# Attention and two expert layers on one core: the fourth pair's last chunks two a turn, and eight early conversion calls

## The chip, the cores and the metric

The kernel runs on one core of a Trainium2 chip. The metric is device time in microseconds (us), the median of several runs. Five engines work side by side: TensorE (PE, whose weight loads are shown as PEld), VectorE (DVE), ScalarE (ACT), GpSimd (POOL) and SyncE (SP). Each takes its own instructions strictly in the order in which they stand in its queue and waits where an input is not ready. DMA transfers are issued from the queues of SP and of ACT (shown as SPq and ACTq).

## What is computed

Attention over 4 batches of 8 heads (576 tokens, head size 64), with a threshold on the scores, then two feed-forward layers over 2304 tokens (width 512, hidden width 2048):

```python
scores = scale * np.matmul(q, k.transpose(0, 1, 3, 2))
thresh = np.max(scores, axis=-1, keepdims=True) - tau
scores = np.where(scores >= thresh, scores, -1000000000.0)
attn = np.exp(scores - np.max(scores, axis=-1, keepdims=True))
attn = attn / (np.sum(attn, axis=-1, keepdims=True) + 1e-09)
x = np.matmul(attn, v)                      # heads side by side: 2304 x 512
h = x @ w_in;  r = np.maximum(h, 0.0)
x = (s * (r * r) + b) @ w_out               # first experts
h = x @ w_in2; g = h * np.tanh(softplus(h))
out = g @ w_out2                            # second experts
```

The weights arrive as 64-bit floats. Each is turned into a high and a low 32-bit part, and a matrix product is made of three products (high by high, high by low, low by high).

## The kernel before

The heads are taken in 16 pairs; four pairs make one batch. A pair has 9 tiles of scores (tile 4 holds rows of both heads), and the generator `attention` runs in turns k, one tile of scores in each: pair k // 9, tile k % 9. Counted from 0, the fourth pair is pair 3. For each tile PE makes the scores S (`scores`, line 346), DVE takes the row maximum while copying them to ns (L350), ACT the exponential (L358), DVE applies the threshold and sums (`finish`, L364), and POOL normalises (L374). Seven turns (LAG) after its scores, chunk c of the pair is transposed on PE into the only buffer T (`weights_t`, L387 and L392) and copied to te by ACT (L398). One T is free again only when its copy has been made. The products with v stand in two runs for each pair (`products_v`, L414 and L417): chunks 1, 4, 0 one turn after the transpose of chunk 6, and chunks 3, 2 one turn after that of chunk 8. Then `split_x` writes the pair's output x as a high part xh (ACT, L425) and a low part xl (DVE, L426). While the scores of pair 4 and 5 are worked on, the transposes of pair 3 are made.

The first experts take a batch once its four pairs have their x: `moe1(0)` needs xh and xl of pairs 0 to 3. Its accumulators h (L516) take nine products from pairs 0 to 2, and the last three from pair 3.

The weights of the first experts are converted in the same time by `split_all`, a chain of `split_w` pieces. A piece loads wraw (L62 on SP while the start-up pool `s2p` is open, L64 on ACT after it was closed), scales it on ACT (L71), puts the bits together on DVE into wa (L73 to L75), casts the high part wp on ACT (L78) and subtracts for the low part (L79, on POOL while `s2p` is open, else on DVE). The result is also stored to memory (L200 on SP). The order of SP is kept behind the pair's moves: L62 is issued after the last move of K or Q made by then (L307). One step of this chain is made at each call `next(w1)`: ahead of the experts at the turns listed in AHEAD (15, 20, 24, 29, 33, 38, 42), and inside `moe1(0)` at every fourth of its yields, the first one among them.

`run` takes attention alone until x of pair 3 exists (in turn 43), then closes `s2p` and interleaves attention and experts by the costs that the generators yield. The order of each engine is not that of the code: a scheduler picks from what is ready, by the position in the code (attention with a priority of 200 positions) and its own estimates of time.

Of the kernel before, what the change touches and what calls it, by code (L numbers as in the profile page):

```python
# [19 lines left out]
class Fused:  # L20
# [409 lines left out]
    def attention(self):  # L430

        nc = self.nc
        self.turn = 0
        N = 9 * self.B * self.NP
        LAG = 7
        for n in "kq":
            self.load_raw(0, n)
        nc.sync.dma_start(self.tau_c, self.tau.partition_broadcast(P))  # L440
        nc.sync.dma_start(self.s_c, self.s.partition_broadcast(P))
        nc.sync.dma_start(self.b_c, self.b.partition_broadcast(P))
        for pr in range(2):
            self.load_raw(pr, "v")
        warm = self.pvp.tile([P, 1024], F32, tag="pv", name="warm")[:, :512]
        self.busy(warm[:, :256], 20)
        self.prep_first(lambda n: self.busy(warm[:, :256], 2 * n))
        fin = todo = None
        tes = {}
        for k in range(N + LAG + 2):  # L450
            pr, ti = divmod(k, 9)
            self.turn = k
            if k < N:
                nxt = self.scores(pr, ti)
                if k < 12:
                    self.busy(warm[:, :256], 3)
                if fin:
                    fin()
                fin = nxt
                yield 550  # L460
                if pr + 1 == self.B * self.NP and ti == 2:
                    self.load_raw(pr, "v")
                if pr + 1 < self.B * self.NP and ti in (1, 4):
                    self.prep_qk(pr + 1, "kq"[ti // 4])
                    if ti == 4 and pr >= 2:
                        with self.tc.issue_after(self.moved):
                            self.load_raw(pr, "v")
                    yield 500
            elif fin:
                fin()  # L470
                fin = None
            j = k - LAG
            run = None
            if todo:
                tp, tc, te = todo
                tes[tc] = te
                if tc == 6:
                    run = self.products_v(tp, (1, 4, 0), tes, True, False)
                    yield 1460
                elif tc == 8:  # L480
                    run = self.products_v(tp, (3, 2), tes, False, True)
                    yield 970
                    self.split_x(tp)
            todo = None
            if 0 <= j < N:
                prj, ci = divmod(j, 9)
                todo = prj, ci, self.weights_t(prj, ci, run)
                yield 550

    def acc(self, name):  # L490
# [297 lines left out]
    def run(self, ctx):  # L788
        tc = self.tc
# [27 lines left out]
        while 3 not in self.x:  # L817
            next(att)
            if self.turn > done and self.turn in AHEAD:
                next(w1)  # L820
# [6 lines left out]
        def first():  # L827

            for i, c in enumerate(self.moe1(0)):
                if i % 4 == 0:  # L830
                    next(w1, None)
                yield c

# [46 lines left out]
        for i, c in enumerate(self.moe1(3)):  # L880
            if 16 <= i < 64 and i % 2:
                next(comb, None)
            elif i >= 64 and i % 4 == 0:
                next(first, None)
# [11 lines left out]


EARLY = 14
AHEAD = [15] + [9 * pr + ti for pr in (2, 3, 4) for ti in (2, 6)]
HALVES = [slice(0, 64), slice(64, 128)]  # L900

N2 = 384
# [48 lines left out]
```

## Time and profile before

| | |
|---|---|
| median of 3 runs | 1115.9 us (1115.75 to 1117.29) |
| the profiled execution | 1117.13 us, of which 1114.9 us are the span from first to last instruction |
| PE busy | 1073.3 us, 96% of the span |
| DVE, ACT, POOL busy | 792.9, 624.9, 285.1 us |
| mean granted TensorE clock | 0.995 |

A busy PE is read with care: the ends of matmuls are modelled, and pipelined matmuls of 288 columns start about every 0.13 us though each is shown with about 0.3 us. What counts is where PE stands idle or has a lower clock. That is for the greater part in the first 130 us, in which attention runs without the experts. From about 132 us on the experts' products fill every hole.

Engines are also slow or fast by their neighbours: the same instruction on DVE or POOL is longer in some places than in others.

### The profile page before, as it was taken

The numbers are of one execution on the slowest core, as the hardware profiler recorded it, in microseconds if no ns is written. First come the engines' busy times: TensorE is split into PE (matmuls) and PEld (weight loads), VectorE is DVE, ScalarE is ACT, GpSimd is POOL, SyncE is SP. The second block draws the span as 40 slices with busy tenths as digits, with TensorE's granted clock in tenths as the row PEclk, the third lists the DMA queues.
The fourth block names the chain that finished last, engine by engine and source line by source line (L and its number), as shares of the span: only waits on it lengthen the run. The fifth ranks groups of instructions, "written<-read, shape, count | busy, mean of one in ns | idle before, by whom it ended". The sixth has DMA issues, their size and how long they took to land.

```text
span 1114.9 us, 21378 instructions
## 1 busy us (share of the span) xinstructions
PE 1073.3 (96%) x7964; PEld 1012.0 (91%) x7964; DVE 792.9 (71%) x1662; ACT 624.9 (56%) x1189; POOL 285.1 (26%) x354
## 2 busy tenths in 40 slices
PE   7987899999999999899999989999999999999998
PEld 6766789999899999879999879999999999999998
DVE  5989699998556777878757656735695468725782
ACT  5777687585486575577746667634453245413451
POOL 4556454355072351344515201100000000000000
PEclk9999999999999999999999999999999999999999
DMA  7577588785666879969855599968998999997783
GB/s 165 132 179 218 149 269 243 237 256 178 196 182 216 259 220 285 306 202 310 305 177 196 184 368 359 357 224 311 349 393 314 364 418 380 342 333 255 261 288 119
DMA packets 141590, 292.69 MB, mean 263 GB/s; under 512 B 52848, under 2 KB 78960, under 8 KB 133168
## 3 DMA queue, kind: packets, MB, share of 16 engines
q1 hardware_dynamic: 127104, 277.93, 74.0%
q10 hardware_dynamic: 14384, 13.40, 4.1%
q8 instruction: 63, 1.03, 0.4%
q14 instruction: 39, 0.32, 0.1%
HBM read 201.85 MB, written 66.58 MB: 241 GB/s over the span
## 4 chain that ended last, share of the span: by engine, by line
PE 70%; DVE 5%; DMA 5%; POOL 2%; issue 2%; ACT 1%; SPq 0%; ACTq 0%; DVEq 0%; POOLq 0%
PE o L761 16%; PE y L516 14%; PE h L516 12%; PE qY L627 7%; PE qX L627 5%; PE qV L627 4%; PE S L346 4%; PE pv L417 3%; PE T L387 3%; DMA wsi<-chli 2%; DMA w<-w 2%; POOL e L374 1%; DMA wso<-chlo 1%; PE pv L414 1%; DVE ns L350 1%
## 5 line engine op out<-in xcount | busy, mean ns | idle before, releaser
L761 PE MATMUL o<-wo,hl 128*128 128x256 f32 x1512 | 177.7, 279 | 0.0
L761 PEld LDWEIGHTS o<-wo,hl 128*128 128x128 f32 x1512 | 177.4, 188 | 0.0
L516 PE MATMUL h<-xh,w 128*128 128x288 f32 x768 | 164.6, 299 | 2.2 <-ACT xh L425 0.7
L516 PE MATMUL y<-gh,w 128*128 128x288 f32 x768 | 164.8, 299 | 1.3 <-DVE y L563 0.8
L374 POOL TENSOR_SCALAR e<-e,st 128x576 f32<-128x576 f32 x128 | 140.5, 1109 | 34.0 <-DVE st L369 24.7
L350 DVE TENSOR_SCALAR_CACHE_REDUCE ns<-S 128x576 f32<-128x576 f32 x144 | 108.0, 752 | 43.9 <-PE S L346 43.0
L358 ACT ACTIVATE e<-ns,st 128x576 f32<-128x576 f32 x128 | 98.9, 775 | 71.1 <-DVE ns L350 67.8
L364 DVE SCALAR_TENSOR_TENSOR e<-ns,st,e 128x576 f32<-128x576 f32 x128 | 114.1, 895 | 26.4 <-ACT e L358 22.9
L516 PEld LDWEIGHTS h<-xh,w 128*128 128x128 f32 x768 | 126.0, 188 | 3.7 <-ACT xh L425 1.2
L516 PEld LDWEIGHTS y<-gh,w 128*128 128x128 f32 x768 | 126.3, 188 | 2.5 <-DVE y L563 1.4
L398 ACT COPY te<-T 128x576 f32<-128x576 f32 x144 | 91.2, 633 | 50.2 <-PE T L392 45.1
L540 POOL TENSOR_TENSOR gl<-rr,gh 128x288 fp32r<-128x288 f32 x96 | 90.3, 952 | 108.9 <-ACT rr L539 107.8
L516 PE MATMUL h<-xl,w 128*128 128x288 f32 x384 | 113.7, 296 | 0.0
L516 PE MATMUL y<-gl,w 128*128 128x288 f32 x384 | 113.4, 295 | 0.0
L346 PE MATMUL S<-KH,Q 128*128 128x288 f32 x320 | 96.2, 318 | 15.7 <-DVE ns L350 7.3
L387 PE MATMUL T<-ident,e 128*128 128x128 f32 x576 | 90.9, 278 | 7.2 <-ACT te L398 5.0
L387 PEld LDWEIGHTS T<-ident,e 128*128 128x128 f32 x576 | 68.0, 142 | 24.2 <-issue 13.6
L346 PE MATMUL S<-KL,Q 128*128 128x288 f32 x320 | 89.9, 297 | 0.0
L627 PE MATMUL qY<-yc,wi 128*128 128x384 f32 x432 | 86.6, 337 | 1.3 <-DVE g L650 1.3
L417 PE MATMUL pv<-te,rawv 128*64 128x288 f32 x576 | 87.8, 423 | 0.0
L346 PEld LDWEIGHTS S<-KH,Q 128*128 128x128 f32 x320 | 60.6, 190 | 21.7 <-DVE ns L350 10.5
L627 PEld LDWEIGHTS qY<-yc,wi 128*128 128x128 f32 x432 | 75.6, 188 | 1.9 <-DVE g L650 1.9
(151 smaller groups left out, 2204.1 us busy)
## 6 DMA issues: line engine op xcount, KB each, us to landing
w<-w SPq DMA_DIRECT2D x96, 512.0 KB, 5.4
wo<-wso SPq DMA_DIRECT2D x42, 1024.0 KB, 7.1
wi<-wsi SPq DMA_DIRECT2D x23, 1024.0 KB, 8.2
wi<-wsi SPq DMA_DIRECT2D x25, 768.0 KB, 8.0
w<-wp SPq DMA_DIRECT2D x32, 512.0 KB, 4.7
wsi<-chli SPq DMA_DIRECT2D x24, 512.0 KB, 4.8
wso<-chlo SPq DMA_DIRECT2D x24, 512.0 KB, 7.1
ycd<-yp SPq DMA_DIRECT2D x14, 768.0 KB, 7.6
```

What stands on the lines that cost most here:

```text
L346: self.scored = nc.tensor.matmul(so, Q[:, c0:c0 + 128], kt[:, ks], start=(i == 0), stop=(i == len(terms) - 1)).ins
L350: nc.vector.tensor_scalar(ns.rearrange("p (h n) -> p h n", h=2), sv, -0.125, 3.0e38, op0=ALU.mult, op1=ALU.min, accum_out=nm[:, c1])
L358: nc.scalar.activation(e, ns, AF.Exp, bias=nm[:, c1], scale=-1.0)
L364: nc.vector.scalar_tensor_tensor(e, ns, nthr[:, c1], e, op0=ALU.is_le, op1=ALU.mult, accum_out=sm[:, c1])
L374: nc.gpsimd.tensor_scalar(t, t, rinv[:, j:j + 1], u[:, j:j + 1], op0=ALU.mult, op1=ALU.add)
L387: nc.tensor.transpose(T[:, i * 128:i * 128 + 128], self.es[pr, i, "pair"][:, o:o + 128], self.ident)
L398: nc.scalar.copy(te, T[:, :576])
L417: ins = self.nc.tensor.matmul(*args, **kw).ins
L516: nc.tensor.matmul(acc[:, :n], w[:, wl, c], rhs[c][xl][:, ts], start=(i == 0), stop=(i == 11))
L540: (nc.vector if b == 3 else nc.gpsimd).tensor_tensor(gl[:, ts], r2, gh[:, ts].bitcast(F32), op=ALU.subtract)
L627: self.nc.tensor.matmul(acc, a, b, start=(first and i == 0), stop=(i == n - 1), skip_group_check=True)
L761: nc.tensor.matmul(bank[p][t], hl[:, gl, j, ts], w[:, 2 * (q % 2) + j, wl], start=(old is None and q + j + k == 0), stop=(q + j + k == 6), ...
```

## The change

Two things are changed. In turns 39 and 40 two chunks are transposed in each (5 and 6, then 7 and 8 of pair 3: the numbers 32 to 35), and none in turns 41 and 42. The first run of products of pair 3 is thereby written in turn 40 (before: 41), the second one in turn 41 (before: 43), and `run` leaves its start-up loop in turn 42. RUNS holds the same two runs as before for every pair, since SOLO is 0. And the conversion is called at eight turns ahead of the experts (15, 19, 23, 27, 31, 35, 39, 42) in place of seven; the call at the first yield of `moe1(0)` is left out, so that the count inside the experts is the same at each later yield.

```diff
-        fin = todo = None
-        tes = {}
+        fin, todo, tes = None, [], {}
+        soon = {39: (32, 33), 40: (34, 35), 41: (), 42: ()} if TWO else {}
+
+        def due(k):
+            return soon.get(k, (k - LAG,) if 0 <= k - LAG < N else ())
+
...
-            j = k - LAG
             run = None
-            if todo:
-                tp, tc, te = todo
+            for tp, tc, te in todo:
                 tes[tc] = te
-                if tc == 6:
-                    run = self.products_v(tp, (1, 4, 0), tes, True, False)
-                    yield 1460
-                elif tc == 8:
-                    run = self.products_v(tp, (3, 2), tes, False, True)
-                    yield 970
+                for chunks in RUNS[tp < SOLO].get(tc, ()):
+                    run = self.products_v(tp, chunks, tes, chunks == RUNS[tp < SOLO][min(RUNS[tp < SOLO])][0], tc == 8)
+                    yield 486 * len(chunks)
+                if tc == 8:
                     self.split_x(tp)
-            todo = None
-            if 0 <= j < N:
+            todo = []
+            for j in due(k):
                 prj, ci = divmod(j, 9)
-                todo = prj, ci, self.weights_t(prj, ci, run)
+                todo.append((prj, ci, self.weights_t(prj, ci, run)))
+                run = None
                 yield 550
...
-                if i % 4 == 0:
+                if i and i % 4 == 0:
                     next(w1, None)
...
-AHEAD = [15] + [9 * pr + ti for pr in (2, 3, 4) for ti in (2, 6)]
+SOLO = 0
+TWO = True
+RUNS = ({6: [(1, 4, 0)], 8: [(3, 2)]}, {5: [(0, 4)], 6: [(1,)], 7: [(2,)], 8: [(3,)]})
+AHEAD = [15, 19, 23, 27, 31, 35, 39, 42]
```

What the scheduler makes of it is seen in the order of the engines. In these rows the number behind a name's last underline is only a counter of tiles; the digit ahead of it is the tile of scores or the chunk (T_6 and te_6 belong to chunk 6).

**Place 1.** ACT where pair 2 ends and the transposes of pair 3 begin. Before (wraw_1290 is the sixth piece of weights):

```order
L398 COPY te_8_1149<-T_8_1143 128x576
L78 CAST wp_0_3_1013<-wa_1417 128x512
L78 CAST wp_1_0_1135<-wa_1605 128x512
L425 CAST xh_1169<-pv_1104 128x576
L398 COPY te_0_1179<-T_0_1173 128x576
L358 ACTIVATE e_2_1272<-ns_2_1269,st_1199 128x576
L398 COPY te_1_1197<-T_1_1191 128x576
L358 ACTIVATE e_3_1309<-ns_3_1306,st_1199 128x576
L71 ACTIVATE wraw_1290<-wraw_1290 128x512
L284 CAST hiq_1343<-tpq_1334 128x640
L398 COPY te_2_1224<-T_2_1218 128x576
```

and now (wraw_1201 is the sixth, wraw_1322 the seventh piece):

```order
L71 ACTIVATE wraw_1201<-wraw_1201 128x512
L398 COPY te_7_1131<-T_7_1125 128x576
L78 CAST wp_1_0_1060<-wa_1449 128x512
L358 ACTIVATE e_0_1220<-ns_0_1217,st_1211 128x576
L358 ACTIVATE e_1_1246<-ns_1_1243,st_1211 128x576
L398 COPY te_8_1149<-T_8_1143 128x576
L71 ACTIVATE wraw_1322<-wraw_1322 128x512
L358 ACTIVATE e_2_1284<-ns_2_1281,st_1211 128x576
L425 CAST xh_1169<-pv_1112 128x576
L398 COPY te_0_1179<-T_0_1173 128x576
L358 ACTIVATE e_3_1309<-ns_3_1306,st_1211 128x576
L284 CAST hiq_1363<-tpq_1354 128x640
```

The sixth piece's scaling has moved from ahead of te_2 of pair 3 to ahead of te_7 of pair 2, and the seventh's now stands ahead of xh of pair 2 and of te_0 of pair 3.

SP at the same place: the moves of K for pair 5 and the load that stands behind them. Before:

```order
L200 DMA w_0_0_1_1412<-wp_0_1_753 128x1024
L200 DMA w_0_0_2_1600<-wp_0_2_873 128x1024
L256 DMA rawk<-in_k_dram 128x8x64
L257 DMA rawk<-in_k_dram 64x2x64
L307 DMA KH_127<-hik_1246 64x576 x2
L307 DMA KH_128<-hik_1246 64x576 x2
L307 DMA KL_129<-lok_1247 64x576
L307 DMA KL_130<-lok_1247 64x576
L62 DMA wraw_1290<-in_moe_w_in_dram 128x4x256
```

and now:

```order
L200 DMA w_0_0_1_1315<-wp_0_1_710 128x1024
L200 DMA w_0_0_2_1444<-wp_0_2_842 128x1024
L256 DMA rawk<-in_k_dram 128x8x64
L257 DMA rawk<-in_k_dram 64x2x64
L307 DMA KH_127<-hik_1258 64x576 x2
L307 DMA KH_128<-hik_1258 64x576 x2
L307 DMA KL_129<-lok_1259 64x576
L307 DMA KL_130<-lok_1259 64x576
L62 DMA wraw_1322<-in_moe_w_out_dram 128x4x256
```

The load behind the moves is now that of the seventh piece. Its place in the queue is the same; the piece is one further on. (Before, the seventh piece, wraw_1419, was loaded behind the moves of Q for pair 5.)

**Place 2.** ACT ahead of the copy of chunk 6 of pair 3, on which the first run of products waits. Before (wraw_1419 is the seventh piece):

```order
L398 COPY te_5_1318<-T_5_1312 128x576
L358 ACTIVATE e_1_1234<-ns_6_1404,st_1199 128x576
L64 DMA wraw_1703<-in_moe_w_out_dram 128x4x256
L358 ACTIVATE e_2_1272<-ns_7_1434,st_1199 128x576
L71 ACTIVATE wraw_1419<-wraw_1419 128x512
L64 DMA wraw_1794<-in_moe_w_out_dram 128x4x256
L398 COPY te_6_1360<-T_6_1354 128x576
```

and now:

```order
L64 DMA wraw_1669<-in_moe_w_out_dram 128x4x256
L398 COPY te_5_1330<-T_5_1324 128x576
L64 DMA wraw_1765<-in_moe_w_out_dram 128x4x256
L358 ACTIVATE e_2_1284<-ns_7_1462,st_1211 128x576
L398 COPY te_6_1338<-T_6_1332 128x576
```

No scaling of weights stands between these copies any more.

**Place 3.** PE at the second run of products of pair 3. The difference from before to now in this stretch is one transpose (chunk 0 of pair 4), which now stands ahead of the run. Before:

```order
L346 MATMUL S_1_1508<-KL_129,Q_125 128x288
L414 MATMUL pv_1378<-te_8_1427,rawv_136 64x288
L417 MATMUL pv_1378<-te_3_1262,rawv_136 64x288
L417 MATMUL pv_1378<-te_7_1397,rawv_136 64x288
L417 MATMUL pv_1378<-te_2_1224,rawv_136 64x288
L387 MATMUL T_0_1451<-ident,e_0_1208 128x128
L276 MATMUL tpk_1519<-ident,rawk 128x64
```

and now:

```order
L346 MATMUL S_1_1520<-KL_129,Q_125 128x288
L387 MATMUL T_0_1467<-ident,e_0_1220 128x128
L392 MATMUL T_0_1467<-ident,E_113 128x128
L414 MATMUL pv_1374<-te_8_1401,rawv_136 64x288
L417 MATMUL pv_1374<-te_3_1274,rawv_136 64x288
L417 MATMUL pv_1374<-te_7_1393,rawv_136 64x288
L417 MATMUL pv_1374<-te_2_1236,rawv_136 64x288
L276 MATMUL tpk_1531<-ident,rawk 128x64
```

In both, S_1 is that of pair 5: the run is neither ahead of the scores that stood ahead of it, nor behind others.

## Rows read from the trace of the kernel before

**Rows 1.** The page: PE's busy tenths in 40 slices of 27.9 us.

```profile
PE   7987899999999999899999989999999999999998
```

**Rows 2.** Stretches: length, busy (instructions) of PE, PEld, DVE, ACT, POOL; clock, DMA, GB/s.

```profile
80.00:100.00 20.00, 15.09 (x114) 11.40 (x112) 19.85 (x47) 15.65 (x29) 12.45 (x10) 1.00 0.67 188
100.00:120.00 20.00, 15.04 (x102) 13.02 (x100) 17.19 (x49) 11.70 (x18) 10.11 (x9) 0.89 0.88 267
...
140.00:160.00 20.00, 20.00 (x158) 18.32 (x157) 19.41 (x35) 17.59 (x41) 13.29 (x14) 1.00 0.92 290
...
108.00:110.00 2.00, 2.00 (x14) 1.98 (x13) 1.77 (x4) 1.13 (x3) 0.00 (x0) 0.71 0.88 202
110.00:112.00 2.00, 2.00 (x11) 1.99 (x10) 2.00 (x8) 1.04 (x2) 0.63 (x1) 0.50 0.82 208
...
120.00:122.00 2.00, 2.00 (x10) 0.96 (x8) 1.30 (x5) 0.00 (x0) 0.69 (x2) 0.50 0.07 18
```

**Rows 3.** PE in order of time: start, us, line, operation, count, [idle before, releaser].

```profile
90.50 2.83 PE L417 MATMUL pv<-te,rawv 128*64 128x288 f32 x21
...
115.53 0.27 PE L392 MATMUL T<-ident,E 128*128 128x128 f32 x1
...
116.03 0.29 PE L346 MATMUL S<-KL,Q 128*128 128x288 f32 x1
118.33 0.46 PE L414 MATMUL pv<-te,rawv 128*64 128x288 f32 x1 [2.01 <-ACT te L398]
...
118.63 4.52 PE L417 MATMUL pv<-te,rawv 128*64 128x288 f32 x21
...
130.16 0.51 PE L516 MATMUL h<-xh,wp 128*128 128x288 f32 x2
```

**Rows 4.** ACT in order of time at places 1 and 2, the same columns.

```profile
101.15 0.64 ACT L398 COPY te<-T 128x576 f32<-128x576 f32 x1
102.99 0.78 ACT L358 ACTIVATE e<-ns,st 128x576 f32<-128x576 f32 x1 [1.21 <-DVE st L368]
...
105.65 0.67 ACT L71 ACTIVATE wraw<-wraw 128x512 f32<-128x512 f32 x1 [0.68 <-DMA wraw<-in_moe_w_in_dram]
...
108.34 0.64 ACT L398 COPY te<-T 128x576 f32<-128x576 f32 x1 [0.23 <-PE T L392]
...
117.10 0.65 ACT L71 ACTIVATE wraw<-wraw 128x512 f32<-128x512 f32 x1 [2.22 <-DMA wraw<-in_moe_w_out_dram]
```

**Rows 5.** SP's DMA issues in order of time; at the end the landing of L62's loads.

```profile
84.85 10.16 SPq L200 DMA_DIRECT2D w<-wp  x3
...
100.54 0.59 SPq L62 DMA_DIRECT2D wraw<-in_moe_w_in_dram  x1
...
111.71 0.59 SPq L62 DMA_DIRECT2D wraw<-in_moe_w_out_dram  x1
...
DMA to landing us min/median/max: 4.1/4.9/5.6
```

**Rows 6.** DVE in order of time, the same columns as in rows 3.

```profile
85.54 1.29 DVE L364 SCALAR_TENSOR_TENSOR e<-ns,st,e 128x576 f32<-128x576 f32 x1
...
89.34 0.80 DVE L364 SCALAR_TENSOR_TENSOR e<-ns,st,e 128x576 f32<-128x576 f32 x1
...
93.99 0.68 DVE L79 TENSOR_TENSOR wp<-wa,wp 128x512 fp32r<-128x512 f32 x1
...
96.65 0.81 DVE L285 TENSOR_TENSOR lok<-tpk,hik 128x640 fp32r<-128x640 f32 x1
```

**Rows 7.** POOL in order of time, the same columns.

```profile
84.23 2.01 POOL L374 TENSOR_SCALAR e<-e,st 128x576 f32<-128x576 f32 x2 [0.81 <-DVE st L369]
...
91.49 1.75 POOL L79 TENSOR_TENSOR wp<-wa,wp 128x512 fp32r<-128x512 f32 x1 [3.42 <-ACT wp L78]
```

**Rows 8.** PE where the third batch of experts begins, the same columns.

```profile
472.58 0.40 PE L346 MATMUL S<-KH,Q 128*128 128x288 f32 x1 [1.64 <-DVE loq L285]
...
473.61 4.52 PE L417 MATMUL pv<-te,rawv 128*64 128x288 f32 x21
```

## The prediction

> **What bounds the kernel now.** First the page's slices of PE. Its digits are 9 nearly everywhere but in the first five, that is up to about 140 us, and three single slices later [rows 1]. So PE sets the end, and time is to be won only where PE stands idle or runs at a lower clock. Second the stretches: from 80 to 120 us PE is busy 15 of 20 us, and from 140 us on 20 of 20, with 158 matmuls [rows 2]. The border between the two is the point at which x of pair 3 is there: the first products that need it stand at 130.16 us [rows 3]. What PE does behind that border is the same in amount before and after the change. So a us by which the border comes sooner, with the same work ahead of it, is a us off the total, as long as no new hole opens later. DVE is full from 80 to 100 us (19.85 of 20) and has some air behind that (17.19 of 20) [rows 2].
>
> Third, what holds the border back, in order of time on PE and ACT. At 118.33 us the first run of products of pair 3 begins, after PE was idle for 2.01 us, and the releaser is the copy te on ACT [rows 3]. In ACT's queue that copy stands behind a scaling of weights (L71, at 117.10 us), for which ACT had waited 2.22 us, because the load of those weights had not landed [rows 4]. It was issued on SP at 111.71 us, and L62's loads land 4.1 to 5.6 us after their issue [rows 5]. So a weight load that nobody needs yet stops the copies of attention, through the order of ACT's queue. Right behind the idle time the granted clock is 0.50, the lower of the two levels (1.2 GHz) [rows 2]: 21 products take 4.52 us, where 21 of the same form took 2.83 us at 90.50 us [rows 3]. A smaller case of the same kind stands earlier: at 105.65 us another scaling waits 0.68 us for its load [rows 4].
>
> **What the change does, part by part.** *The chunks two a turn.* In the order of PE (place 3) the second run still stands behind the scores S_1 of pair 5, now with one transpose (chunk 0 of pair 4) ahead of it that stood behind it. The first run keeps its old neighbours. The scheduler had already taken whatever was ready, so writing the lines two turns sooner moves next to nothing. I count this part as 0: the transpose that is ahead of the run now is missing behind it, and the sum of work ahead of the border is the same.
>
> *The conversion calls.* Nothing is added; pieces come a step sooner. By the border the same seven pieces have been through DVE, so DVE has the same work ahead of it, less one subtraction (L79, 0.68 us at 93.99 us [rows 6]) that has gone to POOL, where one of its kind took 1.75 us [rows 7]. What the calls give is at place 2: no L71 stands ahead of the copy te_6 any more. The transpose of that chunk begins its last step at 115.53 us and ends 0.27 us later, at 115.80 [rows 3]; a copy takes 0.64 us [rows 4], so te is there at 116.44. PE's last product ahead of the run ends at 116.32 (116.03 + 0.29) [rows 3]. So the wait shrinks from 2.01 to between 0.1 and 0.2 us: **1.8 us** gone. If PE does not stand idle, its clock need not fall, and 4.52 - 2.83 = **1.7 us** go as well. Together 3.5 us. What is late next is the PE chain itself (transposes, copies and scores with one T buffer) and DVE behind it.
>
> *Where it costs.* At place 1 the seventh piece's L71 now stands ahead of xh of pair 2 and of te_0 of pair 3, and its load stands in SP behind the moves of K for pair 5. With SP's times of before (issue at 100.54) it would land at 104.6 to 106.1 us [rows 5], while te_0 was copied at 101.15 [rows 4]. But SP comes there sooner. Before, it stood 10.16 us in three stores [rows 5], until the last low part was subtracted at 93.99 [rows 6]; that subtraction is on POOL now, behind another that took 1.75 us from 91.49 [rows 7], and both begin some 3 us sooner since their pieces are a step ahead. And lok of pair 5, which the last moves wait for, stands less far back on DVE: an L350 (0.7 us) and the L79 (0.6) fewer are ahead of it, an L75 (0.65) more, and the rest of the calls' work (1.4 us) has gone into DVE's idle time ahead of 75 us. That makes it about 2 us sooner than 96.65 [rows 6]. I take an issue near 97.5 and a landing between 101.6 and 103.1, which puts te_0 at 103 to 105, 2 to 4 us late. Of this the chain gets back what it wasted further on: between te_0 at 101.15 and te_3 at 108.34 ACT waited 1.21 us for DVE and 0.68 us for a load, and worked 0.67 us on the L71 that has gone from there [rows 4], together 2.6 us. So te_3 comes 0.6 us sooner to 1.4 us later. I take **0**, close to the middle. The bounds: 1.25 us of gain (0.68 for the load and 0.57 until the next instruction began) if the load lands ahead of its turn, and a loss of some 4 us if SP is as late as before.
>
> One rule speaks against the move of the subtraction. In the trace an L364 on DVE takes 1.29 us at 85.54, while POOL is at work, and 0.80 us at 89.34, while it is not [rows 6, 7]. The Trainium skill (SBUF — State Buffer, Who interferes with whom) says that a DVE instruction with two inputs in SBUF and a GpSimd instruction that reads SBUF exclude each other for the whole instruction. The rows agree in direction, though 0.49 us is less than a whole instruction of POOL. By the rule the subtraction on POOL would cost DVE's queue up to its 1.75 us, and the total would be 1.1 us worse after the 0.68 us that DVE no longer spends; by the rows it costs 0.5 us for each DVE instruction that it meets, so with one or two of them nothing. I leave it at 0.
>
> *Later.* Up to pair 9 the order of PE is as before but for a few swaps of neighbours. From there on (some 300 us) the order of the second experts' conversion and of loads differs in many places. PE has holes there at the start of the third batch: 1.64 us idle, and a run at the low clock (4.52 - 2.83 = 1.7 us) [rows 3, 8]. Either may go or come again: 0, with 2 us to either side.
>
> **The sum.** 1.8 + 1.7 + 0 + 0 = 3.5 us less. The profiled execution (1117.13 us, of which the span is 1114.9) is 1.2 us over the median of 1115.9; its own time would become 1113.6, and the median 1115.9 - 3.5 = 1112.4.
>
> **The rivals.**
> *The wait only moves.* ACT stops for the seventh piece ahead of te_0 long enough for PE to idle there and to get the low clock for a run of its work: the 1.8 + 1.7 us are paid there instead. For it: PE has only 15 us of work in the 20 around that place, and the clock was low once already, from about 108.8 us on [rows 2]. Against it: DVE is full there and hides a part of ACT's wait. Time: 1115.9.
> *More goes.* The earlier small stop goes too (1.25 us), and with it the first stretch at the low clock: with mean clocks of 0.71 and 0.50 in two stretches of 2 us, 0.6 + 1.0 = 1.6 us of PE's time [rows 2]. 3.5 + 2.9 = 6.4, or 1109.5. For it: both follow a wait of the same kind. Against it: the new L71 at place 1.
> *Slower.* SP's moves are no sooner than before, the load lands at 106, and te_0 is copied near 107.9 (after 0.6 of L71, 0.7 of an exponential and 0.6 of xh), 6.7 us late; 2.6 are caught up, and behind such a hole PE has the low clock for as long as at 118 (1.7 us): 4.1 + 1.7 - 3.5 = 2.3 us more, 1118.2. It decides from a landing later than about 105 us.
> *It doesn't do what it says.* For the products this is what the order shows, and it is in the forecast. Had they come two turns sooner (a turn is about (118.33 - 90.50) / 9 = 3.1 us [rows 3]), the time would be 1115.9 - 6.2 = 1109.7; no order of PE bears that out, and I give it nothing.
>
> **How the numbers follow.** Forecast 0.52, the wait moves 0.22, more goes 0.16, slower 0.10. A measurement tells some 0.2% (2.2 us) from no change, so faster means under 1113.7 and slower over 1118.1. Faster: 0.46 of the forecast and the 0.16 of more, 0.62. Same: the rest of the forecast and nearly all of the moved wait, 0.27. Slower: 0.11. The range goes from 1108.0 (more goes, with some of the later 2 us) to 1117.0 (the wait moves, and 1 us later); the slower case and the far ends, under 0.2, are left out.
>
> **What would show it.** Right: no idle time of 2 us on PE ahead of the first run of pair 3, the run in 2.8 us at clock 1.00, the first products with x of pair 3 near 126.6 us in place of 130.16, and the same distance kept up to 300 us. Wrong: ACT idle for 3 us or more ahead of an L71 near 100 us; a granted clock of 0.50 in another stretch ahead of the border; or a border that is sooner by 3.5 us and a loss behind 300 us that eats it.

## The result and the profile after

The changed kernel takes 1125.3 us (median of 5 runs, 1121.2 to 1126.5), the kernel before on the same chip 1116.2 us (5 runs, 1115.8 to 1117.3). The ratio is 1.0067, with a 95% interval of 1.0047 to 1.0087: slower, where 1112.4 us and faster were forecast, and outside the range. The profiled execution took 1122.71 us, of which 1120.6 are the span: 2.6 us less than the median, while the profiled execution before (1117.13) lies 0.9 us above its median. The two traces thus differ by 5.6 us, the medians by 9.1, and 3.5 us of the loss can't be looked up in these two traces.

The page's slices of PE, to be held against [rows 1]: the first slices look much as before, and no later one stands out.

```profile
PE   8987999999999999999999999999999999999998
```

PE in order of time (columns as in [rows 3]; the lines behind the edit are one number higher):

```profile
42.40 0.46 PE L414 MATMUL pv<-te,rawv 128*64 128x288 f32 x1 [0.31 <-ACT te L398]
...
92.10 0.43 PE L276 MATMUL tpk<-ident,rawk 128*128 128x64 f32 x2 [3.34 <-DVE ns L350]
...
93.93 3.91 PE L417 MATMUL pv<-te,rawv 128*64 128x288 f32 x21
...
118.63 0.46 PE L414 MATMUL pv<-te,rawv 128*64 128x288 f32 x1 [0.40 <-ACT te L398]
...
118.93 2.83 PE L417 MATMUL pv<-te,rawv 128*64 128x288 f32 x21
...
129.81 0.51 PE L517 MATMUL h<-xh,wp 128*128 128x288 f32 x2
...
723.19 0.40 PE L517 MATMUL h<-xh,w 128*128 128x288 f32 x1 [2.58 <-DMA w<-w]
```

The wait ahead of the first run of pair 3 has gone from 2.01 us to 0.40, and the run takes 2.83 us, as forecast. But the border came 0.35 us sooner (129.81 against 130.16), not 3.5: at 92.10 us stands a new wait of 3.34 us for DVE, and 21 products behind it take 3.91 us, 1.1 us more than at full clock. The stretches (columns as in [rows 2]) show it too:

```profile
80.00:100.00 20.00, 14.11 (x94) 10.53 (x92) 16.73 (x42) 12.03 (x24) 10.05 (x10) 0.91 0.71 195
...
94.00:96.00 2.00, 2.00 (x12) 1.03 (x10) 2.00 (x5) 1.43 (x3) 0.54 (x1) 0.50 0.67 153
...
108.00:110.00 2.00, 0.77 (x5) 0.53 (x5) 2.00 (x3) 1.14 (x3) 1.48 (x2) 1.00 0.85 194
110.00:112.00 2.00, 1.90 (x12) 1.53 (x13) 1.90 (x7) 1.25 (x3) 0.00 (x0) 1.00 0.44 101
...
120.00:122.00 2.00, 2.00 (x19) 1.07 (x16) 1.18 (x4) 0.40 (x1) 0.38 (x2) 1.00 0.32 103
```

PE worked 15.09 us of the first stretch before and 14.11 now. The granted clock of 0.50 (1.2 GHz) that stood at 120 us stands at 94 us now, and the one that stood at 110 us [rows 2] has gone too. DVE and POOL (columns as in [rows 6, 7]) show why:

```profile
88.67 0.08 DVE L364 DVE_READ_ACCUMULATOR e<-ns,st,e 128x1 f32 x1
89.90 1.47 DVE L73 TENSOR_SCALAR wa<-wraw 128x512 int32<-128x512 int32 x1 [1.16 <-POOL wp L79]
91.29 0.74 DVE L350 TENSOR_SCALAR_CACHE_REDUCE ns<-S 128x576 f32<-128x576 f32 x1
91.97 0.08 DVE L350 DVE_READ_ACCUMULATOR ns<-S 128x1 f32 x1
91.97 0.68 DVE L74 SCALAR_TENSOR_TENSOR wa<-wraw,wa 128x512 int32<-128x512 int32 x1
92.57 0.42 DVE L73 TENSOR_SCALAR wa<-wraw 128x512 int32<-128x512 int32 x1
```

```profile
84.27 3.04 POOL L374 TENSOR_SCALAR e<-e,st 128x576 f32<-128x576 f32 x2 [2.94 <-DVE st L369]
87.28 0.83 POOL L374 TENSOR_SCALAR E<-E,st 128x576 f32<-128x576 f32 x1
88.08 3.01 POOL L79 TENSOR_TENSOR wp<-wa,wp 128x512 fp32r<-128x512 f32 x2
```

A piece's L73 now stands on DVE at 89.90 us. The pool `pre` has two buffers for wa, and the one that it needs is still read by a subtraction of POOL, which came to it only after three normalisations of attention. DVE stops for 1.16 us, L73 itself takes 1.47 us where another takes 0.42 at 92.57, and the row maximum L350 that PE waits for stands behind it.

How 0.35 us came of all this is seen at PE's runs of products. Behind the first L414 (42.41 us before, 42.40 now) the second run of pair 2 begins at 59.4 us, where it began at 55.8: 3.6 us late. By the first run of pair 3 all but 0.3 us of that is made good (76.2 against 75.9). The wait of 2.01 us has become 0.40. And an earlier wait of PE for a copy te, 1.88 us before, with a low clock behind it [rows 2], is not there; the longest between these two runs is 1.03 us now, at full clock. The row before:

```profile
107.49 0.66 PE L387 MATMUL T<-ident,e 128*128 128x128 f32 x4 [1.88 <-ACT te L398]
```

The first run of pair 3 then takes 1.7 us less. But between its end and the second run lie 4.6 us now and 3.6 before: the transpose that stands ahead of the second run now (place 3) waits for a copy.

```profile
125.69 0.63 PE L387 MATMUL T<-ident,e 128*128 128x128 f32 x4 [0.96 <-ACT te L398]
```

At place 1 the load was issued at 98.47 us on SP and had landed by 102.79. ACT's rows (columns as in [rows 4]):

```profile
102.79 0.70 ACT L71 ACTIVATE wraw<-wraw 128x512 f32<-128x512 f32 x1 [1.02 <-DMA wraw<-in_moe_w_out_dram]
...
106.12 0.64 ACT L398 COPY te<-T 128x576 f32<-128x576 f32 x1
...
111.48 0.62 ACT L398 COPY te<-T 128x576 f32<-128x576 f32 x1
...
657.69 0.64 ACT L425 CAST xh<-pv 128x576 fp32r<-128x576 f32 x1 [2.08 <-PE pv L417]
...
763.69 0.78 ACT L570 ACTIVATE yo<-y,small 128x576 f32<-128x576 f32 x1 [2.38 <-DVE y L564]
```

The second and third are te_0 and te_3. The last two, xh of the last pair and the last yo of the first experts, bound the fourth batch of experts; before, these two were:

```profile
655.78 0.64 ACT L425 CAST xh<-pv 128x576 fp32r<-128x576 f32 x1 [2.26 <-PE pv L417]
...
757.99 0.78 ACT L569 ACTIVATE yo<-y,small 128x576 f32<-128x576 f32 x1 [2.40 <-DVE y L563]
```

With the first L414 (42.40), the border and the span they cut a trace into four stages, which makes the traces comparable although their starts differ by some 2 us (us, each worked out from these five rows of its trace):

| trace | to the border | border to last xh | fourth batch | rest |
|---|---|---|---|---|
| before | 87.8 | 525.6 | 102.2 | 356.9 |
| before again, three times | 87.3, 89.8, 89.0 | 528.1, 527.7, 527.7 | 101.5, 101.5, 101.8 | 358.7, 358.0, 358.2 |
| changed kernel | 87.4 | 527.9 | **106.0** | 356.9 |
| calls alone | 87.3 | 526.9 | 101.5 | 358.7 |
| chunks alone | 89.2 | 529.2 | **106.2** | 359.1 |
| changed kernel, aligned | 87.2 | 522.7 | 101.8 | 357.3 |
| before, shift 1100 | 84.6 | 528.7 | **106.6** | 356.8 |
| before, shift 2200, twice | 90.1, 88.6 | 521.4, 522.1 | 102.0, 102.2 | 356.2, 357.1 |
| changed kernel, fourth batch spread | 89.0 | 527.0 | 101.7 | 356.5 |
| changed kernel, shift 1100, twice | 87.5, 88.0 | 520.9, 521.3 | 102.3, 102.5 | 358.2, 358.8 |
| changed kernel, 16 early pieces | 87.5 | 532.4 | **108.4** | 358.5 |
| first five calls old | 87.2 | 526.6 | 101.5 | 357.4 |
| first five calls old, shift 2200 | 86.1 | 522.7 | 103.4 | 358.2 |
| third buffer: changed kernel, aligned | 89.6 | 519.2 | 101.9 | 358.0 |
| third buffer: changed kernel, shift 1100 | 88.4 | 518.8 | 102.4 | 357.0 |
| third buffer: before, shift 2200 | 85.5 | 520.8 | 102.2 | 356.2 |

So of the 5.7 us between the two spans 3.8 are in the fourth batch and 2.3 between the border and the last xh (where traces of one order differ by as much), and the stage of the change gave 0.3 us back. The runs behind the rows are told below.

### The profile page after: what moved, and what is told of

Its sections match the earlier page's. It is cut to its first block, busy times and chain, and to the rows that moved or that the text cites. A ratio compares the mean times of both kernels' runs of the same rounds, so it can differ in the third digit from the quotient of the medians.

```text
span 1120.6 us, 21382 instructions
## 1 busy us (share of the span) xinstructions
PE 1076.4 (96%) x7964; PEld 1014.5 (91%) x7964; DVE 800.5 (71%) x1661; ACT 622.1 (56%) x1189; POOL 284.3 (25%) x355
## 3 DMA queue, kind: packets, MB, share of 16 engines
q8 instruction: 63, 1.03, 0.4%
## 5 line engine op out<-in xcount | busy, mean ns | idle before, releaser
L374 POOL TENSOR_SCALAR e<-e,st 128x576 f32<-128x576 f32 x128 | 139.2, 1099 | 36.2 <-DVE st L369 26.7
L358 ACT ACTIVATE e<-ns,st 128x576 f32<-128x576 f32 x128 | 99.1, 775 | 76.2 <-DVE ns L350 73.3
L364 DVE SCALAR_TENSOR_TENSOR e<-ns,st,e 128x576 f32<-128x576 f32 x128 | 113.3, 889 | 35.5 <-ACT e L358 30.8
L350 DVE TENSOR_SCALAR_CACHE_REDUCE ns<-S 128x576 f32<-128x576 f32 x144 | 107.9, 752 | 41.6 <-PE S L346 40.6
L417 PE MATMUL pv<-te,rawv 128*64 128x288 f32 x576 | 87.5, 420 | 0.0
```

The lines of the kernel that those rows point to most:

```text
L350: nc.vector.tensor_scalar(ns.rearrange("p (h n) -> p h n", h=2), sv, -0.125, 3.0e38, op0=ALU.mult, op1=ALU.min, accum_out=nm[:, c1])
L358: nc.scalar.activation(e, ns, AF.Exp, bias=nm[:, c1], scale=-1.0)
L364: nc.vector.scalar_tensor_tensor(e, ns, nthr[:, c1], e, op0=ALU.is_le, op1=ALU.mult, accum_out=sm[:, c1])
L374: nc.gpsimd.tensor_scalar(t, t, rinv[:, j:j + 1], u[:, j:j + 1], op0=ALU.mult, op1=ALU.add)
L417: ins = self.nc.tensor.matmul(*args, **kw).ins
```

## The experiments

Two theories stood at the start. A: the time is lost behind pair 9, because `run` leaves its start-up loop a turn sooner; a turn of scores and transposes (550 + 550) that lay ahead of the interleaving then counts inside it, and all attention behind it stands further back in the written order against the experts. B: the time is lost by the conversion calls and their stop at 88 us. All runs but the three looks were timed in five rounds beside the kernel before; the intervals are at 95%.

### The parts apart

The calls alone (`TWO = False` in the changed kernel):

> The calls part of the change alone: the chunks and the products are written in the old turns. Its order of work equals that of the changed kernel up to the border and that of the kernel before behind pair 9. Theory A (the time is lost behind pair 9, because leaving the start-up loop a turn sooner shifts attention against the experts in the written order): border 0.3 us sooner, no loss behind it, 1115 to 1117 us, ratio 0.999 to 1.001. Theory B (the time is lost because the early conversion calls put a stop on VectorE at 88 us and what follows from it): as slow as the changed kernel, 1121 to 1126 us. Theory C (both are needed): between, 1118 to 1121.

1118.1 us against 1116.5 of before, ratio 1.0006 [0.9993, 1.0020]: no clear difference, with a median 1.1 us above what theory A gave. The chunks alone (old AHEAD, old first call in `first`):

> The chunks two a turn alone: the conversion is called in its old turns. Ahead of the border its order is that of the kernel before, behind pair 9 that of the changed kernel. Theory A (loss from the order behind pair 9): the wait of 2.01 us at 118 us is there again, and the loss too, 1121 to 1126 us, ratio 1.005 to 1.009. Theory B (loss from the early conversion calls): 1115 to 1117 us. Theory C (both are needed): 1117 to 1120.

1126.1 us, ratio 1.0077 [1.0052, 1.0102]. The wait for ACT ahead of the first run was there, 3.31 us, and the fourth batch took 106.2 us. Both parts, with the count set back:

```diff
-        a_done = m_done = 0.0
+        a_done, m_done = -1100.0, 0.0
```

> Both parts of the change, but the count by which attention and experts are interleaved starts 1100 lower for attention, which is what the earlier end of the start-up loop had left undone. Its order ahead of the border is that of the changed kernel but for one copy, behind it that of the kernel before. Theory A (loss from the order behind pair 9): 1114.5 to 1117 us, with the border 0.3 to 0.7 us sooner than before. Theory B (loss from the early calls): 1121 to 1126. If a loss of 2 us or more stays although the first run is at full clock, the early part has a price that the trace ahead of the border does not show.

1118.2 us, ratio 1.0019 [1.0000, 1.0038], above the 1114.5 to 1117 of theory A, far under theory B. Theory A holds for the greater part: the part that does not touch the conversion calls carries the loss, and most of it goes when the order behind the border is that of before. (Its profiled execution, 1112.2 us, was the fastest of 12, so its row in the table is better than its median.) The same shift without the change, in the kernel before (`a_done, m_done = 1100.0, 0.0`):

> The kernel before with one number changed: the count by which attention and experts are interleaved starts 1100 higher for attention, so that attention stands that much further back in the written order from the border on. Nothing ahead of the border changes. Its order behind the border is that of the run with the chunks alone but for a few rows. If this shift alone is the loss of the changed kernel: 1121 to 1127 us, with TensorE waiting 2 us or more for a load of w near 720 us. If the loss needs the earlier products themselves: 1115 to 1118.

1120.6 us, ratio 1.0038 [1.0015, 1.0061], just under the expected range, with a wait of 3.32 us for w at 720.83 us. The shift alone thus makes some 0.4% of the 0.67%; where the rest comes from is not shown by it.

### What the shifted order does

> As before, shifted by 2200. In its order 8 stores of the second experts' conversion stand among the last 20 loads of w, where the kernel before has 9 and the shift by 1100 has 13. Theory D (stores that have moved into the fourth batch, when the DMA engines are full, hold up the loads of w): no wait for w near 720 us, so the loss of 2 to 4 us of the fourth batch is not there, and the time is 1115 to 1122, at least 3 us under the shift by 1100. Theory L (any lag of attention costs, the more the greater): 1125 to 1135.

The edit is `a_done, m_done = 2200.0, 0.0` in the kernel before: 1111.1 us, ratio 0.9957 [0.9937, 0.9978]. Twice the shift is faster than none, so lag as such is not the price. That falls in with theory D, which the next run tested (`EARLY = 16` in the changed kernel):

> The changed kernel with all 16 pieces of the second experts' weights converted ahead of the fourth batch, not 14. Among the last 20 loads of w stand 5 stores, not 13. Theory D: the wait of 2.58 us for w at 723 us goes, the fourth batch takes about 101 us again, not 105, and the time is 3 to 4 us under the changed kernel's, 1120 to 1123, unless VectorE pays for it in attention. Against D: the time stays at 1125, or the fourth batch still takes 105 us.

1132.6 us, ratio 1.0145 [1.0112, 1.0178]: against D as I had put it. The fourth batch took 108.4 us, with a wait of 3.97 us for w, and the stage ahead of it 532.4. The number of stores among the last loads of w is no measure. The stretches of the changed kernel show what is (columns as in [rows 2]: the fourth number from the left is DVE's busy time, the last two are the DMA engines' busy share and GB/s):

```profile
627.69:657.69 30.00, 27.98 (x217) 24.91 (x215) 15.27 (x29) 14.83 (x28) 8.19 (x8) 1.00 0.70 243
677.69:697.69 20.00, 20.00 (x153) 20.00 (x153) 17.39 (x29) 14.02 (x33) 5.58 (x4) 1.00 1.04 407
697.69:717.69 20.00, 20.00 (x153) 20.00 (x152) 14.76 (x29) 12.57 (x29) 4.81 (x4) 1.00 1.03 390
717.69:737.69 20.00, 17.42 (x121) 17.19 (x120) 12.35 (x19) 11.78 (x26) 0.00 (x0) 0.91 1.02 386
```

The same stretches of the kernel before, from 30 us ahead of its last xh on:

```profile
625.78:655.78 30.00, 26.53 (x200) 22.90 (x198) 19.99 (x38) 15.92 (x30) 3.57 (x5) 1.00 0.85 308
675.78:695.78 20.00, 20.00 (x153) 20.00 (x152) 11.03 (x21) 13.73 (x32) 4.49 (x4) 1.00 0.98 377
695.78:715.78 20.00, 20.00 (x153) 20.00 (x153) 14.44 (x27) 12.17 (x25) 4.70 (x4) 1.00 0.94 340
```

In the kernel with 16 early pieces:

```profile
631.62:661.62 30.00, 27.79 (x213) 24.46 (x211) 14.54 (x30) 15.20 (x30) 5.22 (x7) 1.00 0.71 242
661.62:681.62 20.00, 14.61 (x104) 14.15 (x105) 15.24 (x32) 16.61 (x42) 0.00 (x0) 0.98 1.01 372
```

In the 30 us ahead of the fourth batch the changed order has DVE work less (15.27 us busy against 19.99; the conversion's instructions alone 11.1 against 17.6), and the DMA engines move 243 GB/s against 308. The conversion's loads and stores come in the batch itself, where the engines are full for 60 us and PE then waits for w. The other traces fit: in its first 60 us the batch moves 382, 382 and 380 GB/s in the changed kernel, the chunks alone and the shift by 1100, and 351, 348 and 334 before, in the first look at it and with the shift by 2200, which have no such wait. With 16 early pieces the stretch ahead is as idle (242 GB/s) and the wait comes sooner. This suggests that what counts is how much is left for the full stretch. Then the wait must go if the same bytes come later:

```diff
-            if 16 <= i < 64 and i % 2:
+            if 40 <= i < 112 and i % 3 == 0:
                 next(comb, None)
```

> The changed kernel, in which the last two pieces of the second experts' conversion are called later within the fourth batch (in its steps 40 to 111, every third, and not in 16 to 63, every second). Its order is that of the changed kernel up to the fourth batch. Theory D (in the changed order 2.2 MB less have been moved by the DMA engines in the 60 us ahead of the fourth batch, they come in its first 60 us when the engines are full, and the loads of w are late): the wait of 2.6 us for w near 720 us and the low clock behind it go, the fourth batch takes 102 us and not 106, the time is 1121 to 1122. If the wait has another cause: unchanged, 1125.

The edit makes the same 24 calls, and besides takes the place of four calls that prepare the second experts in this batch (steps 72, 84, 96 and 108). 1118.2 us, ratio 1.0019 [1.0001, 1.0037], against 1.0067 without the edit, and better than the 1121 to 1122 expected. In the traces the span falls by 4.1 us. PE shows no wait between 715 and 732 us, and the fourth batch takes 101.7 us:

```profile
678.31:698.31 20.00, 20.00 (x153) 20.00 (x152) 10.88 (x23) 13.99 (x33) 0.00 (x0) 1.00 0.99 352
698.31:718.31 20.00, 20.00 (x153) 20.00 (x152) 17.70 (x29) 13.22 (x27) 2.31 (x2) 1.00 0.94 345
718.31:738.31 20.00, 20.00 (x153) 20.00 (x153) 13.55 (x28) 11.15 (x27) 10.18 (x6) 1.00 0.81 284
738.31:758.31 20.00, 20.00 (x152) 19.90 (x152) 7.26 (x14) 7.60 (x16) 0.00 (x0) 1.00 0.87 341
```

That the conversion calls in the full stretch made the loss of the fourth batch is shown by this. That it is by their bytes is read from PE's releaser, a DMA of w, and from the GB/s: the batch's first 60 us move 350 GB/s now. The ratio stays 0.2% above 1, as with the aligned count, and that rest has no cause shown. Why the scheduler takes fewer conversions ahead of it after a shift of 1100, and why a shift of 2200 also takes some 5 us off the stage before, was not followed up.

### The wait that the forecast took off

Three looks at the unchanged kernel, one run each (1120.0, 1121.3 and 1120.6 us):

> The kernel before, unchanged, for another profile of its first 140 us. The forecast took TensorE's wait of 2.01 us at 118 us and the low clock behind it from one profiled execution. Two kernels with the same order up to the border showed 0.3 and 4.08 us there. If that wait is a draw of when one load lands, it lies anywhere from 0 to 4 us here, and the border 84 to 91 us behind the first products of pair 0; if it is a property of the order, 1.8 to 2.2 us, and 87.5 to 88.

> The same once more: 0 to 4 us for a draw, 1.8 to 2.2 us for a property of the order.

> The same a third time: 0 to 4 us for a draw, 1.8 to 2.2 us for a property of the order.

The rows are PE's first product of that run, in turn from the shift by 1100 and the three looks, with ACT's wait for the load in the last one:

```profile
115.78 0.46 PE L414 MATMUL pv<-te,rawv 128*64 128x288 f32 x1 [0.30 <-ACT te L398]
```

```profile
117.56 0.48 PE L414 MATMUL pv<-te,rawv 128*64 128x288 f32 x1 [3.45 <-ACT te L398]
```

```profile
120.12 0.74 PE L414 MATMUL pv<-te,rawv 128*64 128x288 f32 x1 [4.25 <-ACT te L398]
```

```profile
118.74 0.67 PE L414 MATMUL pv<-te,rawv 128*64 128x288 f32 x1 [4.89 <-ACT te L398]
```

```profile
117.51 0.65 ACT L71 ACTIVATE wraw<-wraw 128x512 f32<-128x512 f32 x1 [5.00 <-DMA wraw<-in_moe_w_out_dram]
```

Ahead of the border these four have one order, and the wait is 0.30, 3.45, 4.25 or 4.89 us: a draw, by when one load lands. From its issue on SP to the L71 it was 4.4 us in the first (110.13 to 114.53) and 7.1 in the last (110.39 to 117.51). The 2.01 us of [rows 3] are another draw, and so are 4.08 and 4.67 us in the two traces of the shift by 2200. The mean of the seven is 3.4 us, so the forecast's draw was a small one; two of the looks lie beyond the 0 to 4 us expected.

### The change ahead of the border by itself

A third buffer for wa, on top of the aligned count (`bufs=3` for the tile wa):

> As the run with the aligned count, and a third buffer for wa, so that VectorE's scaling of piece 4 need not wait for GpSimd's subtraction of an earlier piece at 88 us. If that wait (1.16 us, and 1.05 us of a slow L73 beside it) and the 3.34 us for which TensorE waits at 92 us behind it are what ate the forecast gain, VectorE runs on at 88 us, TensorE keeps its clock at 92 to 98 us, the border comes 2 to 3.5 us sooner than with the aligned count alone, and the time is 1112 to 1114 us. If the wait only gives way to another one on VectorE or GpSimd, the border moves by less than 1 us and the time is that of the aligned count within 1 us.

1115.1 us, ratio 0.9990 [0.9977, 1.0003], 3.2 us under the aligned run beside it. But not as expected. DVE and POOL, and the stretches:

```profile
86.71 1.12 DVE L74 SCALAR_TENSOR_TENSOR wa<-wraw,wa 128x512 int32<-128x512 int32 x1
87.75 1.82 DVE L364 SCALAR_TENSOR_TENSOR e<-ns,st,e 128x576 f32<-128x576 f32 x1
...
89.50 1.75 DVE L75 SCALAR_TENSOR_TENSOR wa<-wraw,wa 128x512 int32<-128x512 int32 x1
91.17 0.41 DVE L73 TENSOR_SCALAR wa<-wraw 128x512 int32<-128x512 int32 x1
```

```profile
87.26 3.44 POOL L79 TENSOR_TENSOR wp<-wa,wp 128x512 fp32r<-128x512 f32 x2
```

```profile
80.00:100.00 20.00, 12.30 (x86) 9.32 (x85) 19.97 (x44) 12.61 (x24) 11.49 (x10) 0.95 0.62 173
100.00:102.00 2.00, 2.00 (x9) 1.00 (x10) 2.00 (x8) 0.62 (x1) 2.00 (x2) 0.50 1.00 239
```

DVE does not stop any more, and is full (19.97 of 20 us); PE waits for it at 95 and 99 us instead (1.52 and 1.98 us), its clock is 0.50 at 100 us, and the border is 89.6 us behind the first products, 2.4 us later than with the aligned count alone. Between the border and the last xh its trace is 3.5 us shorter (519.2 against 522.7), so what the third buffer gives comes behind the border. The spans of these two traces are almost equal (1110.4 and 1110.0 us), so the 3.2 us between the medians are not placed by them.

The stop for the buffer is thus not all of it, but two accounts of the rest stand side by side. One is that the earlier calls put DVE work into a stretch that had no room: up to 90 us DVE has begun 10 instructions of the conversion (L73 to L75, L79) in the changed kernel and 9 with the calls alone, and 7 to 9 in four traces with the old calls. But from 80 to 100 us their number is nearly the same, 15 against 13 to 15. The other is POOL: the two subtractions that now follow each other there lie beside three DVE instructions in the rows above, and these take 1.12, 1.82 and 1.75 us where their kind takes 0.68, 0.80 and 0.68 elsewhere, 2.5 us more together. No run puts these subtractions back on DVE, so the two are not told apart. Leaving the first five calls where they were:

```diff
-AHEAD = [15] + [9 * pr + ti for pr in (2, 3, 4) for ti in (2, 6)]
+AHEAD = [15, 20, 24, 29, 33, 36, 39, 42]
```

(The call at the first yield of `moe1(0)` is left out here too.)

> The kernel before with the chunks in their old turns and the first five conversion calls in their old turns; only the calls 6 and 7 come two turns sooner or at a near turn, and an eighth is added (turns 36, 39, 42). VectorE's order in the full stretch up to 100 us is nearly that of before, and no scaling of weights stands ahead of the sixth copy of pair 3. If the forecast's account of the wait at 118 us is right, and it was eaten only by what the first five earlier calls do at 88 to 97 us: wait gone, first run at full clock, border 2 to 3.5 us sooner, 1112.5 to 1114.5 us. If TensorE is held by VectorE's work there in any order: border within 1 us of before, 1115.5 to 1117.5.

1115.0 us, ratio 0.9980 [0.9959, 1.0000]: no clear difference. The wait at 118 us was gone (0.20 us), and waits of 2.86 us each stood at 97.62 us (for DVE's lok) and 107.20 (for ACT's te). The border came 87.2 us behind the first products, within 1 us of before, as the second case had it. Then the change and the order of the shift by 2200 together (`a_done, m_done = 1100.0, 0.0` in the changed kernel), and three companions:

> The whole change, with the interleaving count 1100 higher for attention. Behind the border its order is that of the kernel before with the shift by 2200, which took 1111.1 us; ahead of it that of the changed kernel. If the order behind the border decides the time, and the change ahead of it is worth under 1 us either way: 1110 to 1112.5 us. If the change ahead of the border costs what the aligned run seemed to show (1.9 us over the kernel before): 1112.5 to 1114. If it gains the forecast 3.5 us: 1107 to 1108.5.

1113.9 us, ratio 0.9987 [0.9972, 1.0003]: in the range of the case in which the change costs.

> As that run, with a third buffer for wa. The third buffer made the aligned run 3.2 us faster in the median (1115.1 against 1118.2). If that is worth the same here: 1107 to 1109 us, the fastest of all. If it was only another order of the work behind the border that came with it: 1110 to 1113.

1110.6 us, ratio 0.9953 [0.9938, 0.9967]: 3.3 us under the run before it, but in the range of another order behind the border, where its trace is 2.1 us shorter (518.8 against 520.9).

> The shift by 2200 together with the old first five conversion calls and only the last ones sooner, which was 1.1 us faster than before in the median on its own. If the two add up: 1109 to 1111 us. If the hole on TensorE only moves with VectorE's work: the time of the shift alone within 1 us, 1110 to 1112.

1113.1 us, ratio 0.9976 [0.9960, 0.9992]: over both ranges, the two do not add up.

> The kernel before with its calls and chunks in their old turns, the interleaving shifted by 2200, and a third buffer for wa. If the conversion calls of the change cost 2 to 3 us by themselves, as four pairs of runs seem to show, this is as fast as or faster than the same with the changed calls: 1107 to 1110 us, ratio 0.991 to 0.996. If the calls cost nothing: 1110 to 1111.

1110.0 us, ratio 0.9938 [0.9918, 0.9958], the lowest median, with the old calls and chunks; its interval overlaps that of the run with the changed calls and the third buffer (0.9953), so with a third buffer no clear cost of the calls is seen. Last, the shift with and without the change on one chip:

> The kernel before with the interleaving shifted by 2200, again, now on the same chip as the next run. Behind the border both have the same order but for a few rows, ahead of it this one has the calls and chunks of before. If the change ahead of the border costs 2 to 3 us, this one is 2 to 3 us under the next run; if it is worth what the traces of the border show (0.4 us sooner on the mean), they agree within 1 us.

> The whole change with the same order behind the border as the run before it. 2 to 3 us over that run if the change costs by itself ahead of the border; within 1 us if it does not; 3 us under it if the forecast's gain is there after all.

1112.3 us, ratio 0.9946 [0.9927, 0.9965], without the change and 1114.8 us, 0.9986 [0.9970, 1.0001], with it. So the whole change costs some 2.5 us also where the order behind the border is nearly the same, as in the earlier pair (0.9957 and 0.9987). Where it costs them is not shown. The traces do not place it ahead of the border: that stage is 88.6 and 90.1 us without the change and 88.0 and 87.5 with it. It is the rest behind the first experts that is longer with it, 358.2 and 358.8 against 356.2 and 357.1, but four traces of the unchanged kernel differ by as much there (356.9 to 358.7).

The clocks do not settle it either. The mean granted clock of the span was 0.998 in 6 of 9 runs without the change and at most 0.997 in 12 with it, and 0.003 of 1112 us is 3.3 us of full speed. But the traced run without the change is one with 0.998, and it has the late load in it, with a wait of 4.67 us on PE. Up to the border its granted clock is 0.98, that of the traced run with the change 0.94, and the latter's border is the sooner one by 0.6 us. The cause of these 2.5 us stays open.

## Why the prediction was wrong

- **What bounds the kernel** held: PE sets the end, and the border is where the early stretch shows.
- **The wait of 2.01 us and the low clock behind it, 3.5 us together.** Both went as the order said, and the border gained 0.35 us. Over all traces of the two orders it is 0.4 us: 88.15 us in the mean of seven with the old order ahead of the border, 87.76 in six of the whole change. The step that failed is the one from "the wait goes" to "the border comes 3.5 us sooner": it counted the chain ahead of the wait as unchanged. "DVE has the same work ahead of it" is true at the border (seven pieces in both) and false at 90 us, where the conversion is 10 instructions far and not 7. The sum looked at ACT, SP and place 2, and gave the moved pieces no place on DVE and no buffer. There DVE stops for a buffer that POOL still reads, PE waits 3.34 us and runs 1.1 us longer at the low clock, and the second run of pair 2 is 3.6 us late. The border misses the forecast's 126.66 us by 3.15: 2.1 at the first run of pair 3, which begins at 118.63 and not near 116.5, and 1.0 between it and the second. The size was moreover taken from one execution: the wait was a draw between 0.3 and 4.9 us.
- **Place 1, 0.** The load came near the forecast: issue at 98.5 (97.5 said), landed by 102.8 (101.6 to 103.1 said), so the slower rival, a load that lands after 105 us, did not happen. But te_0 came at 106.1 (103 to 105 said), behind a wait of 1.43 us for DVE in ACT's queue, and te_3 at 111.48, 3.1 us later than before, where 0.6 us sooner to 1.4 later was said. So the chain was late where the wait had been: the forecast had te_6 at 116.44 us, it was there at 118.58.
- **The subtraction on POOL, 0.** Too low. By the order of the pieces the first of the two subtractions at 88.08 us holds the buffer (it was on POOL before as well), and the second is the one that was moved there. Beside the second an L73 took 1.47 us, not 0.42. It was not put back on DVE alone, so its share is open.
- **The chunks two a turn, 0.** The order of PE ahead of the border hardly moved, as said, but the transpose that now stands ahead of the second run costs it about 1 us. And this part carries the larger loss, 1.0077 by itself, since it ends the start-up loop sooner.
- **Later, 0 with 2 us to either side.** Mis-sized, and the larger failure: the fourth batch alone cost 3.8 to 4.4 us against the 102.2 of the first trace, in each of the three traces with that order, because fewer conversions ran ahead of it and PE waited for w (2.58 us in the changed kernel). I had seen that conversion and loads stand in other places from some 300 us on, and put a bound on it from holes at the third batch [rows 8], not from the stage in which the DMA engines are full.
- **The rivals.** "The wait only moves" has nearly the right result for the early stretch by a wrong mechanism: DVE for a buffer of POOL, not ACT for a load. "More goes" came in half: the earlier low clock went, and its gain was eaten as well. No rival looked behind the border. Of the signs of being wrong, a granted clock of 0.50 in another stretch ahead of the border came true (at 94 us), and so did the loss behind 300 us, though the border ahead of it was not 3.5 us sooner.

What stays open is 3.5 us of the 9.1 between the medians, which the two traces do not hold, and the 2.5 us that the change costs with the faster order behind the border.

## What to carry to other kernels

Where conversion runs in the gaps of an engine, the same work up to some later point says nothing about the stretch before it: give each moved piece its place on every engine that it passes, and ask which slower engine still reads the buffer that it needs. Where a loop's end feeds a count that interleaves two chains, as here, a change of one turn can re-order what stands behind it, and the stage in which the transfers are full is the one to look at first. A wait for a load that is read from one execution may be a draw, as here: look at two or three before it goes into a sum.

## What the runs showed of the hardware

The time of one load in one order, from issue to use, went from 4.4 to 7.4 us between executions (7.4 in the second look, 111.49 to 118.89), and with it PE's wait from 0.3 to 4.9 us. The unchanged kernel's runs went from 1110.9 to 1123.6 us in the later comparisons, where the first five lay within 1.6 us.

The forecast took 0.5 us for a DVE instruction that meets POOL's reads. An L364, 0.80 us when alone [rows 6], took 1.82 us at 87.75 beside two subtractions on POOL that began at 87.26 and took 1.72 us each on the mean. Had it stood until the first of them ended at about 88.98 and then taken 0.80, it would have ended at 89.78; it ended at 89.57. The Trainium skill (SBUF — State Buffer, Who interferes with whom) says that such a pair contends, and that contention there is an exclusive lock. Read as a lock for one whole instruction, this row agrees within 0.2 us. Here the forecast's half a microsecond was too little. It isn't always DVE that pays: in the changed kernel an L364 took 0.81 us at 84.56, though two L374 on POOL are shown from 84.27 on, which took 1.52 us each on the mean there and 1.0 us in the row at 84.23 of [rows 7].
